# Loading and transposing the first head pair in halves, ahead of the centroids, in a clustered-attention and gated-feed-forward kernel

## The chip, the cores and the metric

The kernel runs on one core of a Trainium2 chip. The time is the device time of one execution in microseconds (us). Before the change the median of 7 runs is 344.58 us (343.99 to 345.71). A further execution was recorded by the hardware profiler; all durations and moments below come from that one, counted from the start of its span. The engines are TensorE (PE; its weight loads are listed apart as PEld), VectorE (DVE), ScalarE (ACT), GpSimd (POOL) and SyncE (SP), which here only issues DMAs.

## What is computed

Attention with routing by clusters, then a gated feed-forward network. There are 4 batches of 8 heads, 768 tokens, head size 64 and 16 centroids for each head. In short:

```python
q_assign = argmax(normalised(q) @ normalised(centroids).T)      # for each token and head, one of 16
k_assign = argmax(normalised(k) @ normalised(centroids).T)
scores   = q @ k.T / 8, and -1e9 where q_assign != k_assign
x        = softmax(scores) @ v                                  # heads side by side: 3072 x 512
xn       = x / sqrt(mean(x*x) + 1e-6) * rms_g
out      = (silu(xn @ w_gate) * (xn @ w_val)) @ w_out           # 512 -> 1536 -> 512
```

## The kernel before, in words

Heads are worked in 16 pairs. Each pair goes through a preparation whose parts `prep_parts` (L179) returns, and then through two *slots* of the main loop, one for each head.

The parts are named T0, T1, T2, T3, CAST, SP, TR, MX, CMP, SCL, BACK, PLACE and CASTV (L471). T0 to T3 are `t_group(g)` (L184) with g = 2 x head + side, side 0 for q and 1 for k: T0 is q of the first head, T1 is k of the first head, T2 is q of the second head, T3 is k of the second. Each makes three transposes of 128x128 float32 on TensorE (L194) into a PSUM tile tp, and then one copy of tp to one slice of the SBUF tile qk32 (L198 on VectorE, L200 on ScalarE; the line `on_dve` says which). A transposed group has tokens of even position in partitions 0 to 63 and of odd position in 64 to 127, so that CAST writes each group in two halves ("par" 0 and 1) as bfloat16 into aug, the operand of the score matmuls. For the first pair CAST reads PSUM (L211 on VectorE, L213 on ScalarE); for the others GpSimd does it (L217).

SP (`assign`, L225) multiplies the four slices of qk32 with the block-diagonal centroids cbd, four tiles side by side in the array, into PSUM (sp). TR, MX, CMP, SCL and BACK (L240 to L261) are five VectorE instructions, each reading what the one before wrote: transpose, maximum over the centroids, compare, scale, transpose back to ohT. PLACE (L264) sends ohT by four DMAs of 24 KB into rows 64 to 79 of the aug tiles; for the first pair one is issued by ScalarE, one by SyncE and two by GpSimd. So the score matmul sees both q·k and a large negative term where the clusters differ. CASTV copies v to bfloat16 on GpSimd (L222).

The order of everything is written out by hand (`manual_schedule`): an engine runs its instructions in the order of the program text. Before the main loop stand the loads, the centroid chain and the preparation of the first three pairs.

The loads: centroids on ScalarE's queue (L95); then on SyncE's queue q and k of pairs 0, 1 and 2 (each 384 KB: both heads), v of pair 0, and q of pair 3, which waits until T0 and T2 of pair 0 have been read because its buffer is that of pair 0 (three buffers for each of q, k and v).

The centroid chain (L139 to L146): sum of squares on VectorE, square root as a power on GpSimd (c_nm, L140), then on VectorE a reciprocal, a multiply-and-add, an add of 2e-6, a reciprocal and a scaling into c2. `put_centroids` (L148) transposes c2 on TensorE (c_ps) and copies it into cbd in two VectorE instructions (L152, L153), one for each half of the partitions, all eight heads at once.

`keep_warm(n)` (L126) issues n matmuls of 128x512 zeros, whose result is not used. The start in the program's order (L473 to L483):

```python
w_ps = keep_warm(9)
p0[T0](); p0[T2]()
keep_warm(2, w_ps)
put_centroids()
p0[T1](); p0[T3]()
p0[CAST]()
keep_warm(1, w_ps)
for i in (SP, TR, MX, CMP, SCL, BACK, PLACE):
    p0[i]()
```

Then come T0 to T3 of pair 1, two more loads, three warm-up matmuls, T0 to T3 and the casts around pair 2, five more warm-up matmuls, and the main loop (L546). A step of that loop makes a ninth of one slot's scores (L301; in the early slots three ninths at once, "scw"), their exponential on ScalarE (L304), a group of the product with v for the slot before (L315), and pieces of the feed-forward network of the batch before (L403, L436), and calls the parts of later pairs' preparation at steps listed in L496 to L541.

Of the kernel before, what the change touches and what calls it, by code (L numbers as in the profile page):

```python
# [8 lines left out]
F32 = mybir.dt.float32  # L9
BF16 = mybir.dt.bfloat16  # L10
AX = mybir.AxisListType.X
ALU = mybir.AluOpType
# [7 lines left out]
def kernel(  # L20
# [12 lines left out]
    nc = tc.nc  # L33
    B, H, S, D = q.shape
    NC = centroids.shape[1]
    DM, DF = moe_w_gate.shape
    P = 128
    ST = S // P
# [16 lines left out]
    const = ctx.enter_context(tc.tile_pool(name="const", bufs=1))  # L55
    ld = ctx.enter_context(tc.tile_pool(name="ld", bufs=3))
# [20 lines left out]
    loads = {}  # L77
# [9 lines left out]
    def load_pair(pi, kinds=range(3)):  # L87
        for kind in kinds:
            load_part(pi, kind)
# [3 lines left out]
    c_in = const.tile([P, D + 1], F32, name="c_in")  # L93
    nc.vector.memset(c_in[:, D:D + 1], 1e-15)
    nc.scalar.dma_start(out=c_in[:, 0:D], in_=centroids.rearrange("h c d -> (h c) d"))  # L95
    for pi in range(3):
        load_pair(pi, (0, 1))
    load_part(0, 2)
    load_part(3, 0)
# [6 lines left out]
    cbd = const.tile([P, H, NC, 2], F32, name="cbd")  # L106
# [19 lines left out]
    def keep_warm(n, w_ps=None):  # L126
        if w_ps is None:
            w_ps = ps_first.tile([P, CH], F32, name="w_ps", tag="f")
        for _ in range(n):
            nc.tensor.matmul(w_ps, lhsT=zeros[:, 0:P], rhs=zeros, start=True, stop=True)  # L130
        return w_ps
# [3 lines left out]
    c_ss = const.tile([P, 1], F32, name="c_ss")  # L135
    c_nm = const.tile([P, 1], F32, name="c_nm")
    c_t = const.tile([P, 1], F32, name="c_t")
    c2 = const.tile([P, 2, D], F32, name="c2")
    nc.vector.scalar_tensor_tensor(c_sq, c_in, 1.0, c_in, op0=ALU.mult, op1=ALU.mult, accum_out=c_ss)  # L139
    nc.gpsimd.tensor_tensor(c_nm, c_ss, half, op=ALU.pow)  # L140

    nc.vector.reciprocal(c_t, c_nm)
    nc.vector.scalar_tensor_tensor(c_t, c_t, c_ss, c_nm, op0=ALU.mult, op1=ALU.add)
    nc.vector.tensor_scalar_add(c_t, c_t, 2e-6)
    nc.vector.reciprocal(c_t, c_t)
    nc.vector.tensor_scalar_mul(c2, c_in[:, 0:D].unsqueeze(1).to_broadcast([P, 2, D]), c_t)  # L146

    def put_centroids():  # L148
        c_ps = ps_pv.tile([P, P], F32, name="c_ps", tag="acc")
        nc.tensor.transpose(c_ps, c2[:, :, :].rearrange("p a d -> p (a d)"), ident_f)  # L150
        c_pv = c_ps[:, :].rearrange("p (h c) -> p h c", c=NC)
        nc.vector.tensor_copy(cbd[0:D, :, :, 0], c_pv[0:D, :, :])  # L152
        nc.vector.tensor_copy(cbd[D:P, :, :, 1], c_pv[D:P, :, :])  # L153


    wg = const.tile([P, DC, DF], BF16, name="wg")
# [16 lines left out]
    def t_tile(name):  # L173
        pool, tag = ps_t, "t"
        if "wide" not in late:
            pool, tag = ps_first, "f"
        return pool.tile([P, HS], F32, name=name, tag=tag)

    def prep_parts(pi):  # L179
        st = pi % NSET  # L180
        qk32 = [None]
        state = {}

        def t_group(g):  # L184
            a, side = divmod(g, 2)
            if qk32[0] is None:
                qk32[0] = prep.tile([P, 4, HS], F32, name="qk32", tag="qk32", bufs=3)
            if pi == 2 and g > 1:
                tp = ((ps_t, ps_pv)[g - 2]).tile([P, HS], F32, name="tp", tag=("t", "acc")[g - 2])
            else:  # L190
                tp = t_tile("tp")
            src = loads[pi, side]
            for i in range(TH):
                nc.tensor.transpose(tp[:, i * P:(i + 1) * P], src[:, a, i * P:(i + 1) * P], ident_f)  # L194
            dst = qk32[0][:, g, :]
            on_dve = (g in (0, 3) if pi == 0 else g == 3 if pi == 2 else pi < 7 or g % 2)
            if on_dve:
                nc.vector.tensor_copy(dst, tp)  # L198
            else:
                nc.scalar.copy(dst, tp)  # L200
            state[g] = tp

        def casts():
            if pi == 0:
                for g in (0, 2, 1, 3):
                    a, side = divmod(g, 2)
                    for par in range(2):
                        dst = aug[0][a][0:D, side, par * HS:(par + 1) * HS]
                        src = state[g][par * D:(par + 1) * D, :]
                        if g == 3:  # L210
                            nc.vector.tensor_copy(dst, src)  # L211
                        else:
                            nc.scalar.copy(dst, src)  # L213
                return
            for a in range(2):
                for par in range(2):
                    nc.gpsimd.tensor_copy(aug[st][a][0:D, :, par * HS:(par + 1) * HS],  # L217
                                          qk32[0][par * D:(par + 1) * D, 2 * a:2 * a + 2, :])

        def casts_v():  # L220
            v_in = loads[pi, 2]
            nc.gpsimd.tensor_copy(vbf[st][:, :, :, 0:D],  # L222
                                  v_in[:, :, :].rearrange("p a (t d) -> p a t d", d=D))

        def assign():  # L225
            h0 = 2 * (pi % NP)
            if pi == 1:
                sp = ps_pv.tile([P, HS], F32, name="sp", tag="acc")
            else:
                sp = t_tile("sp")  # L230
            for j in range(4):
                side, a = divmod(j, 2)
                nc.tensor.matmul(sp[32 * j:32 * j + 32, :], lhsT=cbd[:, h0 + a, :, :].rearrange("p c r -> p (c r)"),  # L233
                                 rhs=qk32[0][:, 2 * a + side, :], start=True, stop=True,
                                 tile_position=(0, 32 * j))
            state["sp"] = sp

        def oh_tr():
            tr = prep.tile([P, HS], F32, name="tr", tag="tr")
            nc.vector.transpose(tr, state["sp"])  # L240
            state["tr"] = tr[:, :].rearrange("p (n c r) -> p n r c", c=NC, r=2)

        def oh_max():
            mx = small.tile([P, TH * 4, 2], F32, name="mx", tag="mx")
            nc.vector.tensor_reduce(mx, state["tr"], axis=AX, op=ALU.max)  # L245
            state["mx"] = mx

        def oh_cmp():
            oh = prep.tile([P, HS], BF16, name="oh", tag="oh")
            nc.vector.tensor_tensor(oh[:, :].rearrange("p (n c r) -> p n r c", c=NC, r=2), state["tr"],  # L250
                                    state["mx"].unsqueeze(3).to_broadcast([P, TH * 4, 2, NC]), op=ALU.is_ge)
            state["oh"] = oh

        def oh_scale():
            oh = state["oh"]
            nc.vector.tensor_scalar(oh[0:64, :], oh[0:64, :], scalar1=1.0, scalar2=MASK,
                                    op0=ALU.subtract, op1=ALU.mult)

        def oh_back():
            ohT = prep.tile([P, HS], BF16, name="ohT", tag="ohT")  # L260
            nc.vector.transpose(ohT, state["oh"])  # L261
            state["ohT"] = ohT

        def place():  # L264
            ohT = state["ohT"]
            for a in range(2):
                for side in range(2):
                    r = 32 * (2 * side + a)
                    eng = nc.sync
                    if pi == 0 and (side or not a):  # L270
                        eng = nc.gpsimd if side else nc.scalar
                    elif pi == 1 and (a or side):
                        eng = nc.gpsimd
                    eng.dma_start(out=aug[st][a][D:KA, side, :].rearrange("c (r n) -> c r n", r=2),
                                  in_=ohT[r:r + 2 * NC, :])

        return [lambda: t_group(0), lambda: t_group(1), lambda: t_group(2), lambda: t_group(3), casts, assign, oh_tr, oh_max, oh_cmp, oh_scale, oh_back, place, casts_v]


# [190 lines left out]

    T0, T1, T2, T3, CAST, SP, TR, MX, CMP, SCL, BACK, PLACE, CASTV = range(13)  # L471
    p0, p1, p2, p3 = (prep_parts(pi) for pi in range(4))
    w_ps = keep_warm(9)  # L473
    p0[T0]()
    p0[T2]()
    keep_warm(2, w_ps)
    put_centroids()
    p0[T1]()
    p0[T3]()
    p0[CAST]()  # L480
    keep_warm(1, w_ps)
    for i in (SP, TR, MX, CMP, SCL, BACK, PLACE):
        p0[i]()  # L483
    for i in (T0, T1, T2, T3):
# [3 lines left out]
    w_ps = keep_warm(3)  # L488
# [113 lines left out]
```

## Time and profile before

| | before |
|---|---|
| median of 7 runs | 344.58 us (343.99 to 345.71) |
| the profiled execution | 344.8 us |
| its span | 343.0 us |
| TensorE busy | 333.8 us (97%), 2957 matmuls |
| ScalarE busy | 225.8 us (66%) |
| VectorE busy | 222.4 us (65%) |
| GpSimd busy | 88.5 us (26%) |
| DMA | 34.99 MB, mean 102 GB/s |
| first score matmul starts | 14.89 us |

The profile has a page of totals, the chain of waits that ended last, followed back from the last instruction (line by line: start, length, what), a timeline of merged groups of instructions (start, length, engine, line, operation, operands, count, and in brackets the idle time before it with what ended it), and a list of DMA issues with the time from issue to landing. A group "x6" is six instructions in a row; its length runs from the first start to the last end. Matmuls overlap: a transpose is listed as 0.27 us or 0.42 us long, while the next one starts sooner. L numbers are lines of the kernel before the change.

### The profile page before, as it was taken

To read this page: it belongs to the slowest core of one execution; us is meant where nothing else is said; L and a number is where in the kernel's file an instruction comes from. 1 tells how busy PE (TensorE), PEld (TensorE's weight loads), DVE (VectorE), ACT (ScalarE), POOL (GpSimd) and SP (SyncE) were. 2 spreads that over 40 slices of the span, in tenths; PEclk is the share of its full clock that TensorE was granted. 3 is DMA by queue.
4 is the path that set the end of the run, shared out by engine and by line. 5 is a ranking of instruction groups with operands and counts; after the bars stand their busy time and mean duration, and the time that the engine had idled before them with its cause. 6 is when DMAs were issued, how large, how long until landed. Compare 5 with 4: busy or idle time off the path is not lost.

```text
span 343.0 us, 7541 instructions
## 1 busy us (share of the span) xinstructions
PE 333.8 (97%) x2957; PEld 203.7 (59%) x2957; DVE 222.4 (65%) x464; ACT 225.8 (66%) x392; POOL 88.5 (26%) x121
## 2 busy tenths in 40 slices
PE   8898999999999999999999999999999999999996
PEld 4556666667666565665656566566665655555553
DVE  4777787698765768766465668775555587655540
ACT  3588999978777586866767677777778343323322
POOL 1578696066441124231211304020000001000000
PEclk9999999999999999999999999999999999999999
DMA  7647999909843126161401002120000030300012
GB/s 263 211 143 247 235 249 245 266 14 156 224 152 110 71 52 176 44 183 39 151 28 42 32 11 68 45 56 32 32 1 32 32 78 32 78 31 31 32 62 92
DMA packets 36771, 34.99 MB, mean 102 GB/s; under 512 B 13520, under 2 KB 33664, under 8 KB 36736
## 3 DMA queue, kind: packets, MB, share of 16 engines
q1 hardware_dynamic: 30560, 29.62, 28.0%
q0 software_dynamic: 5984, 4.84, 9.0%
q8 instruction: 23, 0.38, 0.5%
q14 instruction: 12, 0.10, 0.1%
q10 hardware_dynamic: 192, 0.06, 0.1%
HBM read 28.61 MB, written 6.29 MB: 102 GB/s over the span
## 4 chain that ended last, share of the span: by engine, by line
PE 88%; DVE 7%; ACT 2%; issue 1%; DMA 1%; POOLq 0%; POOL 0%; DVEq 0%; ACTq 0%
PE gp L403 18%; PE vp L403 18%; PE dp L436 18%; PE sc L301 12%; PE acc L315 9%; PE tp L194 5%; PE sp L233 3%; PE scw L301 3%; ACT pT L304 2%; PE w_ps L130 1%; DVE oh L250 1%; DVE qk L198 1%; DVE tr L240 1%; DVE mx L245 1%; DMA aug<-ohT 1%
## 5 line engine op out<-in xcount | busy, mean ns | idle before, releaser
L304 ACT ACTIVATE pT<-sc 128x512 bf16<-128x512 f32 x192 | 113.7, 598 | 44.4 <-PE sc L301 44.0
L412 DVE SCALAR_TENSOR_TENSOR uu<-th,gp 128x384 f32<-128x384 f32 x96 | 53.1, 553 | 66.1 <-ACT th L408 65.9
L403 PE MATMUL vp<-xnT,wv 128*128 128x384 bf16 x384 | 78.1, 325 | 0.2 <-DVE gvT L418 0.2
L403 PE MATMUL gp<-xnT,wg 128*128 128x384 bf16 x384 | 78.1, 325 | 0.1
L436 PE MATMUL dp<-wo,gvT 128*128 128x512 bf16 (+1 forms) x300 | 75.9, 370 | 0.0
L408 ACT ACTIVATE th<-gp 128x384 f32<-128x384 f32 x96 | 47.3, 493 | 43.3 <-PE gp L403 40.6
L315 PEld LDWEIGHTS <-pT 128*128 128x128 bf16 x1152 | 57.0, 97 | 28.8 <-issue 2.5
L301 PE MATMUL sc<-aug 80*128 80x512 bf16 (+1 forms) x256 | 72.9, 326 | 0.0
L217 POOL CAST aug<-qk 64x768 bf16<-64x768 f32 x60 | 52.1, 869 | 53.5 <-DVE qk L198 36.9
L315 PE MATMUL acc<-vbf,pT 128*128 128x65 bf16 x1152 | 63.0, 194 | 0.6 <-ACT pT L304 0.2
L418 DVE TENSOR_TENSOR gvT<-uu,vp 128x384 bf16<-128x384 f32 x96 | 52.6, 548 | 6.1 <-PE vp L403 0.8
L403 PEld LDWEIGHTS <-wg 128*128 128x128 bf16 x384 | 37.2, 97 | 30.0 <-issue 0.4
L304 ACT ACTIVATE pT<-scw 128x1536 bf16<-128x1536 f32 x32 | 44.9, 1457 | 5.9 <-PE scw L301 5.5
L403 PEld LDWEIGHTS <-wv 128*128 128x128 bf16 x384 | 37.1, 97 | 18.6 <-issue 0.5
L436 PEld LDWEIGHTS <-gvT 128*128 128x128 bf16 x300 | 29.1, 98 | 24.4
L301 PEld LDWEIGHTS <-aug 80*128 80x128 bf16 x384 | 33.2, 97 | 16.3 <-issue 6.2
L198 DVE COPY qk<-tp 128x384 f32<-128x384 f32 x41 | 22.3, 552 | 15.4 <-PE tp L194 15.3
L301 PE MATMUL scw<-aug 80*128 80x512 bf16 (+1 forms) x128 | 26.0, 325 | 0.6 <-DMA aug<-ohT 0.4
L369 DVE SCALAR_TENSOR_TENSOR xn<-x,ir,g_b 128x512 bf16<-128x512 bf16 x24 | 20.2, 858 | 5.0 <-POOL ir L361 3.9
L222 POOL CAST vbf<-v_in 128x768 bf16<-128x768 f32 x16 | 13.4, 836 | 35.0 <-issue 34.6
L194 PE MATMUL tp<-ident_f,k_in 128*128 128x128 f32 x96 | 16.3, 282 | 2.5 <-DVE qk L198 2.2
L325 DVE TENSOR_TENSOR x<-acc,inv 128x384 bf16<-128x384 f32 x32 | 17.8, 558 | 1.1
(62 smaller groups left out, 196.2 us busy)
## 6 DMA issues: line engine op xcount, KB each, us to landing
q_in<-in_q_dram SPq DMA_DIRECT2D x16, 384.0 KB, 5.1
k_in<-in_k_dram SPq DMA_DIRECT2D x16, 384.0 KB, 5.4
v_in<-in_v_dram SPq DMA_DIRECT2D x16, 384.0 KB, 5.4
out_dram<-ob SPq DMA_DIRECT2D x23, 256.0 KB, 2.0
wg<-in_moe_w_gate_dram POOLq DMA_DIRECT2D x4, 384.0 KB, 8.8
wv<-in_moe_w_val_dram POOLq DMA_DIRECT2D x4, 384.0 KB, 10.7
wo<-in_moe_w_out_dram POOLq DMA_DIRECT2D x4, 384.0 KB, 7.2
aug<-ohT SPq DMA_DIRECT2D x58, 24.0 KB, 1.9
```

Source lines behind the costliest of these rows:

```text
L194: nc.tensor.transpose(tp[:, i * P:(i + 1) * P], src[:, a, i * P:(i + 1) * P], ident_f)
L198: nc.vector.tensor_copy(dst, tp)
L217: nc.gpsimd.tensor_copy(aug[st][a][0:D, :, par * HS:(par + 1) * HS], qk32[0][par * D:(par + 1) * D, 2 * a:2 * a + 2, :])
L301: nc.tensor.matmul(sc[:, o:o + n], lhsT=ag[:, 1, kc * P:(kc + 1) * P], rhs=ag[:, 0, qo:qo + n], start=True, stop=True)
L304: nc.scalar.activation(pts[slot][:, j * CH:(j + nch) * CH], sc[:, :nch * CH], ACT.Exp, scale=scale)
L315: nc.tensor.matmul(acc[:, TORD[g], :], lhsT=pts[slot][:, kc * S + g * P:kc * S + (g + 1) * P], rhs=vb[:, a, TORD[kc], :], start=(kc == 0), ...
L369: nc.vector.scalar_tensor_tensor(st["xn"][:, tl, :], x_t[b][:, t, :], st["ir", m][:, tl:tl + 1], g_b, op0=ALU.mult, op1=ALU.mult)
L403: nc.tensor.matmul(pt[:, :HS], lhsT=w[:, dc, fc * P:(fc + 1) * P], rhs=xnT[b, m][:, :, dc, :], start=(dc == 0), stop=(dc == DC - 1))
L408: nc.scalar.activation(th, pt[:, :HS], ACT.Tanh, scale=0.5)
L412: nc.vector.scalar_tensor_tensor(uu, th, 1.0, pt[:, :HS], op0=ALU.add, op1=ALU.mult)
L418: nc.vector.tensor_tensor(gvT[half][:, fc, :], uu, pt[:, :HS], op=ALU.mult)
L436: nc.tensor.matmul(dp, lhsT=gvT[hf][:, f, tl * P:(tl + 1) * P], rhs=wo[:, f, cols], start=(f == 0), stop=(f == FC - 1))
```

## The change

1. The first pair's q and k are loaded in four DMAs of 192 KB, one for each head and side, instead of two of 384 KB. The k of head 0 is issued by ScalarE behind the centroids, the other three by SyncE.
2. T0, T1, T2, T3 of pair 0 run in this order, all ahead of `put_centroids`, with 7 warm-up matmuls before T0, one after it, and 2 before SP (12 to 10 in all).
3. Of pair 0, only T3 is copied to qk32 by VectorE (T0 was too), and the casts run in the order of the groups; VectorE makes one cast (the second half of T3's group) instead of two, ScalarE seven instead of six.
4. `put_centroids` copies c_ps to cbd in four instructions: heads 0 and 1 for both halves of the partitions, then heads 2 to 7.
5. In the centroid chain, 2e-6 is added to c_nm by GpSimd (into c_ne), and the multiply-and-add takes c_ne; the add on VectorE is dropped.

```diff
-    for pi in range(3):
+
+    for kind, src in enumerate((q, k)):
+        loads[0, kind] = ld.tile([P, 2, ST * D], F32, name=("q_in", "k_in")[kind], tag=("q_in", "k_in")[kind])
+    for a in range(2):
+        for kind, src in enumerate((q, k)):
+            eng = nc.scalar if kind and not a else nc.sync
+            eng.dma_start(out=loads[0, kind][:, a, :], in_=src[0, a].rearrange("(p t) d -> p (t d)", p=P))
+    for pi in range(1, 3):
         load_pair(pi, (0, 1))
...
+    c_ne = const.tile([P, 1], F32, name="c_ne")
+    nc.gpsimd.tensor_scalar(c_ne, c_nm, scalar1=2e-6, scalar2=None, op0=ALU.add)
     nc.vector.reciprocal(c_t, c_nm)
-    nc.vector.scalar_tensor_tensor(c_t, c_t, c_ss, c_nm, op0=ALU.mult, op1=ALU.add)
-    nc.vector.tensor_scalar_add(c_t, c_t, 2e-6)
+    nc.vector.scalar_tensor_tensor(c_t, c_t, c_ss, c_ne, op0=ALU.mult, op1=ALU.add)
     nc.vector.reciprocal(c_t, c_t)
...
-        nc.vector.tensor_copy(cbd[0:D, :, :, 0], c_pv[0:D, :, :])
-        nc.vector.tensor_copy(cbd[D:P, :, :, 1], c_pv[D:P, :, :])
+        for hs in (slice(0, 2), slice(2, H)):
+            nc.vector.tensor_copy(cbd[0:D, hs, :, 0], c_pv[0:D, hs, :])
+            nc.vector.tensor_copy(cbd[D:P, hs, :, 1], c_pv[D:P, hs, :])
...
-            on_dve = (g in (0, 3) if pi == 0 else g == 3 if pi == 2 else pi < 7 or g % 2)
+            on_dve = (g == 3 if pi == 0 else g == 3 if pi == 2 else pi < 7 or g % 2)
...
-                for g in (0, 2, 1, 3):
+                for g in (0, 1, 2, 3):
...
-                        if g == 3:
+                        if g == 3 and par:
...
-    w_ps = keep_warm(9)
+    w_ps = keep_warm(7)
     p0[T0]()
+    keep_warm(1, w_ps)
+    p0[T1]()
     p0[T2]()
+    p0[T3]()
+    put_centroids()
+    p0[CAST]()
     keep_warm(2, w_ps)
-    put_centroids()
-    p0[T1]()
-    p0[T3]()
-    p0[CAST]()
-    keep_warm(1, w_ps)
     for i in (SP, TR, MX, CMP, SCL, BACK, PLACE):
         p0[i]()
```

## The prediction

> **What bounds the kernel now.** I read the page first, then the chain of waits from the start to 40 us, then the timeline, and last the DMA view issue by issue.
>
> ```profile
> span 343.0 us, 7541 instructions
> ...
> PE 88%; DVE 7%; ACT 2%; issue 1%; DMA 1%; POOLq 0%; POOL 0%; DVEq 0%; ACTq 0%
> ```
>
> TensorE carries 88% of the chain, and the change takes no matmul out of the main loops. So the change can pay only in the start-up, before the first score matmul, by as much as it moves that matmul. The start of the chain:
>
> ```profile
> 1.18 4.02 PE w_ps L130 x9
> 5.20 1.28 PE tp L194 x6
> 6.48 0.47 PE w_ps L130 x2
> 6.95 0.11 PE c_ps L150
> 7.06 0.67 PE tp L194 x6
> 7.73 0.02 issue
> 7.75 0.56 DVE qk L198
> 8.31 0.46 DVE aug L211
> ...
> 8.78 0.56 DVE aug L211
> ...
> 9.37 0.59 DVE tr L240
> ...
> 12.10 2.66 DMA aug<-ohT
> ...
> 14.89 0.81 PE scw L301 x4
> ```
>
> To be seen: up to 7.73 TensorE sets the pace. Then VectorE copies the last transposed group, casts it twice, and only then begins the run tr, mx, oh, oh, ohT (9.37 to 12.07), whose result goes by DMA into aug and releases the first scores at 14.89. From 9.37 on nothing in this chain is edited, so I price the change by the start of tr. The assignment matmuls (sp) end at 9.20, only 0.17 before tr.
>
> ```profile
> 4.94 1.14 PEld L194 LDWEIGHTS tp<-ident_f,q_in 128*128 128x128 f32 x6 [0.65 <-POOL c_nm L140]
> ...
> 7.10 0.28 DVE L152 COPY cbd<-c_ps 64x128 f32<-64x128 f32 x1 [0.63 <-PE c_ps L150]
> 7.40 0.31 DVE L153 COPY cbd<-c_ps 64x128 f32<-64x128 f32 x1
> 7.75 0.56 DVE L198 COPY qk<-tp 128x384 f32<-128x384 f32 x1
> 7.80 2.93 ACT L213 CAST aug<-tp 64x384 bf16<-64x384 f32 x6
> 7.86 1.34 PE L233 MATMUL sp<-qk,cbd 128*32 128x384 f32 x8
> ```
>
> The first transposes start at 4.94. The releaser that is printed is c_nm, but the transposes read q_in, and the DMA view has its landing:
>
> ```profile
> q_in<-in_q_dram SPq DMA_DIRECT2D x1, 384.0 KB, 4.1
> ```
>
> Issued at 0.73, it landed at 4.83, 0.11 before the weight load. The k load (issued 1.24, 4.6 us) landed at 5.84, the next q at 6.94. That is one 384 KB load per 1.0 us, 396 GB/s in the stretch from 3.5 to 4.5: the transfers queue for bandwidth.
>
> **The change, part by part.**
>
> *Loads.* The first q and k become four loads of 192 KB: q head 0 (SP), k head 0 (ACT, behind c_in), q head 1 and k head 1 (SP). Bytes are the same, so all four are down by 5.84. If they are served in the order of issue, they land half a microsecond apart: 4.33, 4.83, 5.34, 5.84. ACT's extra issue costs 0.44 (as c_in's) and pushes its table load from 1.19 to about 1.65; hidden, since ACT first works at 6.52. SP issues one load more before the second pair (0.5 us each): hidden, since those transfers wait for bandwidth and land a microsecond apart until 12.3 whenever they are issued; without that backlog it would cost 0.5 on pair 1.
>
> *TensorE.* Two spacings of one shape matter. The nine warm-up matmuls take 4.02 for the first 0.63 long: 0.424 apart. The five at 13.27 take 1.24 with 0.38 for one: 0.215 apart. Transposes stand likewise 0.214 apart in the q group (1.49 less 0.42, over 5) and 0.109 in the k group (0.82 less 0.27, over 5). The rate doubles between 6.27 and 6.57, in the two matmuls between those groups; I put it at 6.35. Seven warm-ups end at 1.18 + 7 x 0.424 = 4.15. T0 then waits for its half: 4.33 + 0.16 (as 4.83 to 4.99 now) = 4.49, after 0.34 idle. T0 to 5.13; one warm-up to 5.56; T1 (landed 4.83) to 6.20; T2 (landed 5.34) crosses the change of rate, to 6.58; T3 (landed 5.84) starts its last transpose at 6.80 and is done at 7.07. Now this last group is done at 7.71, so **T3 is 0.64 earlier**: 0.50 from the landing, the rest from two warm-ups and the centroid transpose (0.51 + 0.11) that no longer stand ahead of it, less the slow rate at which T1 now runs. Those three go behind T3 and end by 7.3, hidden by VectorE's work.
>
> *VectorE.* Now: copy (7.75; the next instruction follows 0.47 on), two casts (0.55 + 0.56), 0.03, tr: 1.62. After: copy 0.47, four cbd copies, one cast 0.56, 0.03. A cbd copy of 128 columns takes 0.30, a cast of 384 columns 0.55; a line through both gives 0.20 for 32 columns and 0.27 for 96, so the four cost 0.94. Bounds: 0.14 each if columns alone counted (0.60 in all), 0.30 each at worst (1.20). I take 0.94. So tr starts 2.00 after the copy: 7.07 + 0.04 + 2.00 = **9.11 against 9.37, a gain of 0.26**. The dropped cast and the two copies moved in nearly cancel the moved transposes. Cover: sp needs the first two cbd copies, done at 7.11 + 0.47 + 0.40 = 7.98; it takes 0.85 from one start when all operands are there (16 matmuls later in the trace: 15.63, 0.85), so it ends at 8.88, before VectorE is free. That it need not wait for all four copies is read from qk: sp starts at 7.86 while another slice of the same tile is being written until 8.31.
>
> *ScalarE.* It takes three copies and seven casts instead of two and six: copies at about 5.4, 6.4, 6.9, then 7 x 0.49, done near 10.7 as now. Its aug DMA waits for ohT (11.8) and is not delayed; the margin is 1.1, and with it gone one cast costs 0.49. Heads 0 and 1 of the casts in another order: nothing, slot 0's four end by 9.3.
>
> *Centroid chain.* One VectorE add of 0.19 start to start goes, but the next instruction now waits for a GpSimd add. Nearest row: GpSimd's 128x3 add at L360, 0.23. c_nm ends at 4.84, so the sum is there at about 5.2 where VectorE arrives at 5.07: zero net, bounds -0.19 and +0.3. Either way c2 is ready by 6.3 and c_ps starts after 6.9: hidden.
>
> *Later.* SP's next loads (at 12.88 and 13.46) and GpSimd's casts stand behind the aug DMAs and move with them. The main loop from 14.89 is released by those DMAs, so I carry the 0.26 to the end unchanged. The profiled execution took 344.8, span 343.0 plus 1.8 around it, 0.2 over the median: 344.8 - 0.26 = 344.54, and on the median 344.58 - 0.26 = **344.3**.
>
> **Two rules of the skill that speak against it.** The Trainium skill, DMA: Bandwidth & Descriptors, Issuing engines are not separate DMA queues, says that DMAs from several engines interleave on the same 16 DMA engines and that spreading them saves only issue time; by it the sum is rival B's, no gain. The Trainium skill, TensorE: Matmul & The Clock Gate, Part 1, has a free-running activity window of 3413 ns that must be busy before the clock doubles; the granted clock reads 1.00 throughout here, so only the spacings show it, and what an idle 0.34 does to such a window no trace here shows. By that rule the sum could be rival C's.
>
> **The rivals.**
>
> *B, the halves share the engines.* If k head 0 on ACT's queue takes every second turn from q head 0, both land at 4.83. T0 starts at 4.99 as now, T1 ends at about 6.53, T3 at 7.35, tr at 9.39: no gain, 344.6. For it: while c_in and q run together, c_in is not held back, though issued beside q (it lands 3.1 us after its issue). Against: k head 0 is issued 0.45 later.
>
> *C, slower: the rate of TensorE doubles later.* Now nothing interrupts TensorE from 1.18 to the doubling at 6.35. After, it stands idle for 0.34 (0.84 under B). If that idle time keeps the slow rate past 7 us, the loss begins there: T2 and T3 at 0.214, done at 7.69; copy 7.73; first two cbd copies 8.60; sp at half rate 1.70, to 10.35; tr at 10.42, 1.05 late: 345.6. With B's landing about 0.46 more: 346.1. For it: the slow rate holds for 5.2 us of unbroken work now. Against: later gaps (0.58 before 12.56, 0.38 before 14.89) leave the spacing fast.
>
> *D and E, collisions in the loop.* On the chain at 27.17 the oh compare took 1.12 instead of its median 0.59, and the scale at 28.33 took 0.73 instead of 0.25, beside GpSimd's casts. That is 1.02 us that a shift of 0.26 can undo (D: 344.3 - 1.0 = 343.3) or make a second time (E: 345.3; under B 345.6).
>
> *F, sp waits for all four cbd copies.* They end at 8.52; 0.05 + 0.85 + 0.07 gives tr at 9.49, 0.12 late: 344.7.
>
> **How the numbers follow.** Forecast 0.28, B 0.18, C 0.25, D 0.17, E 0.08, F 0.04. The bound of 0.3%, about what a measurement of this kernel can tell from no change, is 1.03 us: faster is below 343.55, slower above 345.61. Faster is D: 0.17. Slower is C but for its mildest tenth, and E where it meets B: 0.25. Within: 0.58. The range takes in D below and C alone above with the copies' bounds (0.3 either way): 343.2 to 345.9, leaving out C with B and what meets twice.
>
> **What would show it.** Right: the first q group's weight load near 4.5, the k group after one warm-up near 5.6, T3's copy on VectorE near 7.1, four cbd copies behind it of 0.2 to 0.27, tr near 9.1, first scores near 14.6. B: first weight load near 4.9. C: transposes of T2 and T3 still 0.21 apart, sp over 1.3 long. D or E: durations of oh between 20 and 35 us. The forecast falls if the first scores come earlier but a wait further on (the third pair's transposes behind GpSimd's casts at 30 us) takes it back, or if q head 0 lands after 4.9.

## The result and the profile after

| | before | after |
|---|---|---|
| median | 344.86 us (31 runs, 343.98 to 346.94) | 347.21 us (12 runs, 345.97 to 347.77) |
| the profiled execution, its span | 344.8 us, 343.0 | 347.42 us, 345.6 |
| ratio, 95% interval | | 1.0061 (1.0046 to 1.0076) |
| tr of pair 0 starts | 9.37 us | 10.67 us |
| first score matmul starts | 14.89 us | 16.18 us |
| mean granted clock of TensorE | 1.000 | 0.995 |

The kernel is slower by 0.6%, outside the range of the prediction. (The ratio is formed over the runs; the two medians alone would give 1.0068.) Two parts can be told apart at once in the profiles: the first scores come 1.29 us later, and the span is 2.6 us longer, so a second 1.3 us is lost after that. Line numbers from here on are those of the changed kernel, nine higher in most places (L249 is tr, L220 and L222 are the casts of pair 0 on VectorE and ScalarE, L310 the scores).

The page's totals and the chain's shares of the changed kernel:

```profile
span 345.6 us, 7541 instructions
...
PE 86%; DVE 8%; ACT 3%; issue 1%; DMA 1%; POOLq 0%; POOL 0%; DVEq 0%; ACTq 0%
```

The chain of waits of the changed kernel, from the start to the first scores (start, length, what):

```profile
1.18 3.17 PE w_ps L137 x7
4.34 0.64 PE tp L203 x3
4.98 0.43 PE w_ps L137
5.41 0.44 PE tp L203 x3
...
5.88 0.86 ACT qk L209 x2
6.74 0.36 ACT aug L222
...
9.57 0.48 ACT aug L222
...
10.08 0.56 DVE aug L220
...
10.67 0.59 DVE tr L249
...
13.39 2.65 DMA aug<-ohT
...
16.18 0.81 PE scw L310 x4
```

Before the change this chain went from TensorE straight to VectorE. Now ScalarE stands between them from 5.88 to 10.05, with its copies and casts, and VectorE's cast comes after the last of them. The timeline shows why:

```profile
6.53 0.56 DVE L207 COPY qk<-tp 128x384 f32<-128x384 f32 x1 [0.97 <-PE tp L203]
6.62 3.43 ACT L222 CAST aug<-tp 64x384 bf16<-64x384 f32 x7
7.01 0.17 DVE L161 COPY cbd<-c_ps 64x32 f32<-64x32 f32 x1
7.19 0.20 DVE L162 COPY cbd<-c_ps 64x32 f32<-64x32 f32 x1
7.42 0.25 DVE L161 COPY cbd<-c_ps 64x96 f32<-64x96 f32 x1
...
7.53 0.85 PE L242 MATMUL sp<-qk,cbd 128*32 128x384 f32 x8 [0.50 <-DVE cbd L162]
7.68 0.26 DVE L162 COPY cbd<-c_ps 64x96 f32<-64x96 f32 x1
...
10.08 0.56 DVE L220 CAST aug<-tp 64x384 bf16<-64x384 f32 x1 [2.13 <-ACT aug L222]
```

To be seen: VectorE has done the four cbd copies at 7.94, and the assignment matmuls are done at 8.38; tr could start then. But in VectorE's order its half cast of T3's group stands ahead of tr, and VectorE is idle for 2.13 us ahead of that cast, until ScalarE's seventh cast is over at 10.05. Both read the same PSUM tile, though not the same half of it: ScalarE's cast takes partitions 0 to 63, VectorE's 64 to 127. And ScalarE comes to this tile only at 9.57; from 7.94 to then it casts other groups. So what VectorE waits for is its turn, and not a memory that is being read.

The second part lies near 33 us. The wait of TensorE ahead of it, and then TensorE in steps of two microseconds (length, busy time and instructions, granted clock, share of DMA, GB/s), in the changed kernel:

```profile
32.07 0.55 PE L203 MATMUL tp<-ident_f,k_in 128*128 128x128 f32 x3 [1.63 <-DVE qk L207]
```

```profile
31.00:33.00 2.00, 0.93 (x11) 0.95 0.84 229
33.00:35.00 2.00, 2.00 (x19) 0.50 1.00 326
35.00:37.00 2.00, 2.00 (x26) 0.70 0.48 146
```

From 32.8 on TensorE is granted half its clock for 3.41 us, soon after 1.63 us in which it had stood waiting for a VectorE copy. Before the change the same wait is there and the clock stays at 1.00:

```profile
30.87 0.55 PE L194 MATMUL tp<-ident_f,k_in 128*128 128x128 f32 x3 [1.66 <-DVE qk L198]
```

```profile
31.70:33.70 2.00, 2.00 (x31) 1.00 0.86 259
```

Of the 12 runs after the change 9 have a mean clock of 0.995 and a median of 347.26; the other three, at 1.000, have 346.00. A mean of 0.995 is what one such stretch makes: half of 3.41 us is 0.5% of 345.6. Where the stretch lies can be seen only in the profiles, in this one and in two of the variants below; in all three it comes right after TensorE's idle time there.

### The profile page after: what moved, and what is told of

It is laid out like the page before. It is cut to its first block, busy times and chain, and to the rows that moved or that the text cites. A ratio compares the mean times of both kernels' runs of the same rounds, so it can differ in the third digit from the quotient of the medians.

```text
span 345.6 us, 7541 instructions
## 1 busy us (share of the span) xinstructions
PE 334.5 (97%) x2955; PEld 204.2 (59%) x2955; DVE 222.2 (64%) x463; ACT 226.5 (66%) x394; POOL 88.1 (25%) x122
## 4 chain that ended last, share of the span: by engine, by line
PE 86%; DVE 8%; ACT 3%; issue 1%; DMA 1%; POOLq 0%; POOL 0%; DVEq 0%; ACTq 0%
PE gp L412 18%; PE vp L412 18%; PE dp L445 17%; PE sc L310 12%; PE acc L324 8%; PE tp L203 5%; PE sp L242 3%; PE scw L310 3%; ACT pT L313 2%; DVE oh L259 1%; DVE qk L207 1%; PE w_ps L137 1%; DVE tr L249 1%; DVE mx L254 1%; DVE ohT L270 1%
## 5 line engine op out<-in xcount | busy, mean ns | idle before, releaser
L310 PE MATMUL sc<-aug 80*128 80x512 bf16 (+1 forms) x256 | 73.0, 327 | 0.0
L310 PEld LDWEIGHTS <-aug 80*128 80x128 bf16 x384 | 33.5, 98 | 16.4 <-issue 6.3
L310 PE MATMUL scw<-aug 80*128 80x512 bf16 (+1 forms) x128 | 26.9, 334 | 0.5 <-DMA aug<-ohT 0.4
L209 ACT COPY qk<-tp 128x384 f32<-128x384 f32 x24 | 11.2, 481 | 11.3 <-PE tp L203 7.1
```

The source lines that it names most:

```text
L310: nc.tensor.matmul(sc[:, o:o + n], lhsT=ag[:, 1, kc * P:(kc + 1) * P], rhs=ag[:, 0, qo:qo + n], start=True, stop=True)
```

## The experiments

Theory W: the first part is that one wait. Theory K: the second part is the stretch of half clock that follows TensorE's idle time near 30 us. The main rival of W is that the loads or the new order of the transposes cost the time. Each time stands against the kernel before on the same chip; "full clock" are runs whose mean granted clock is 0.998 or more.

**Both halves of T3's group on VectorE.**

```diff
-                        if g == 3 and par:
+                        if g == 3:
```

> The changed kernel, but both halves of T3's group are cast by VectorE, as before the change; all else is as changed. Theory W (the loss of the start is one wait: VectorE's half cast waits for ScalarE's seventh cast, and tr stands behind it): the wait goes, the casts follow the cbd copies at 7.95, tr starts near 9.1 instead of 10.67, the first scores near 14.6 instead of 16.2; if the granted clock is 1.00 throughout, about 344.6 us, else 1.2 more. Rival L (the loss comes from the loads and the order of the transposes): first scores stay near 16, time near 347.

345.31 us against 344.48, ratio 1.0022 (1.0003 to 1.0042). The wait is gone: the cbd copies end at 8.37, two casts follow at 8.38, tr starts at 9.54 and the first scores at 15.06. That is 1.1 earlier than in the changed kernel, and 0.45 later than expected, because T3 waited 0.35 for the second k load and its copy starts at 6.96 instead of 6.53. Six of the 12 runs are at 0.995; the six at full clock have 344.66, still 0.3 above those of before on that chip (344.37). W holds; L falls as the cause of the 1.3 us, though the loads do have a part in the 0.45.

**The kernel before, with the split cast alone.**

```diff
-                        if g == 3:
+                        if g == 3 and par:
```

> The kernel before, with one line of the change alone: VectorE casts only the second half of T3's group, ScalarE the first half (seven casts instead of six, in the old order). Theory W: ScalarE's seven casts run from 7.8 to 11.2, VectorE's waits for the last, tr starts near 11.8 instead of 9.37, the first scores near 17.3; 2.4 us slower than before, about 347.3, and more if a stretch of half clock is added. Rival L: VectorE casts once instead of twice, tr near 9.3 (the assignment matmuls end at 9.2), time as before, 344.9.

347.50 us against 344.48, ratio 1.0079 (1.0051 to 1.0108). One line alone, which takes work off VectorE, costs as much as the whole change does. In its timeline:

```profile
7.66 3.42 ACT L213 CAST aug<-tp 64x384 bf16<-64x384 f32 x7
...
11.11 0.56 DVE L211 CAST aug<-tp 64x384 bf16<-64x384 f32 x1 [2.94 <-ACT aug L213]
11.70 0.58 DVE L240 STREAM_TRANSPOSE tr<-sp 128x384 f32<-128x384 f32 x1
```

VectorE is idle for 2.94 us where the kernel before was idle for nothing; tr is at 11.70 (11.8 expected), the first scores at 17.20. Three of 6 runs are at 0.995 (348.52), three at full clock (346.44).

**All eight casts on ScalarE.**

```diff
-                        if g == 3 and par:
+                        if False:
```

> The changed kernel, but ScalarE makes all eight casts of the first pair and VectorE none. Theory W: no wait of VectorE on ScalarE is left, tr starts when the assignment matmuls end, near 8.45, the first scores near 14.0 (0.9 earlier than before the change), about 344.0 us; ScalarE's last cast ends near 10.6, ahead of ohT at 11.2. Rival L: first scores near 16, time near 347. A second rival (the later loop takes the gain back, or its stretch of half clock stays): first scores at 14.0 and the time still 344.9 or more.

345.76 us against 344.48, ratio 1.0018 (0.9998 to 1.0037). Read alone the median says that taking the wait out gains 1.5 us and no more; but 8 of 12 runs are at 0.995 (345.90) and the four at full clock have 343.76, 0.6 below the full-clock runs of before on that chip (344.37). In the profile tr waits for nothing but the assignment matmuls, and ScalarE's eighth cast is over at 11.04, ahead of ohT:

```profile
7.13 3.91 ACT L222 CAST aug<-tp 64x384 bf16<-64x384 f32 x8
...
9.28 0.58 DVE L249 STREAM_TRANSPOSE tr<-sp 128x384 f32<-128x384 f32 x1 [0.50 <-PE sp L242]
```

tr is 0.8 later than the 8.45 expected, since in this execution TensorE's rate doubled late: T1, T2 and T3 (5.21, 5.88, 6.51) each take 0.82 to 0.87, against 0.49 to 0.63 in the profile of the changed kernel. The same is seen in the kernel before: by the trace's record of the clock the rate doubles at 6.43 in its profile and at 5.33 in that of its filled control further down, with tr at 9.37 and at 8.83, though the two programs differ only in matmuls that run at 28.95 and later. Single profiles are to be compared with this half microsecond in mind.

**The first half on VectorE, the second on ScalarE.**

```diff
-                        if g == 3 and par:
+                        if g == 3 and not par:
```

> The changed kernel, but VectorE casts the first half of T3's group and ScalarE the second, so that of the two it is ScalarE that comes later. The work of each engine is that of the changed kernel. Theory W (the wait is one of order between two engines that read the same PSUM tile): VectorE's cast follows the cbd copies at 7.95, tr near 8.55, the first scores near 14.1, about 344.1 us if the clock stays at 1.00. Rival L, or a rival by which one cast more on ScalarE is what costs: first scores near 16, time near 347.

344.24 us against 344.48, ratio 0.9997 (0.9975 to 1.0019); eight runs at full clock have 344.01. The work on each engine is that of the changed kernel; only which engine comes later is turned round, and 3 us of median go (4 of 12 runs are still below full clock). The cast follows the cbd copies without a gap:

```profile
8.56 0.55 DVE L220 CAST aug<-tp 64x384 bf16<-64x384 f32 x1
...
9.05 0.58 DVE L249 STREAM_TRANSPOSE tr<-sp 128x384 f32<-128x384 f32 x1
```

First scores at 14.56 (14.1 expected; T3 waited 0.66 for the second k load). Two rivals fall with it: that a seventh cast on ScalarE costs the time, and that the loads do.

**The idle time near 30 us filled, in three kernels.** Four matmuls of zeros are issued after the score chunk of step 27, into the score tile that the next chunk overwrites:

```diff
+    def fill(n):
+        late["next"] = late["wide"].tile([P, WCH * CH], F32, name="scw", tag="scw")
+        for _ in range(n):
+            nc.tensor.matmul(late["next"][:, 0:CH], lhsT=zeros[:, 0:P], rhs=zeros, start=True, stop=True)
...
-            sc = late["wide"].tile([P, WCH * CH], F32, name="scw", tag="scw")
+            sc = late.pop("next") if "next" in late else late["wide"].tile([P, WCH * CH], F32, name="scw", tag="scw")
...
+    at(27, lambda: fill(4))
```

> The changed kernel with four matmuls of 512 columns of zeros more, issued after the score chunk of loop step 27, into the score tile that the next chunk overwrites: they lie in the stretch near 30 to 32 us in which TensorE waits for a VectorE copy. Theory K (beside the wait, most of the changed kernel's runs lose 1.2 us more to 3.4 us of half clock that follow this idle stretch): the granted clock is 1.000 in every run, the median near 346.0, 1.5 over before, first scores still at 16.2. Rival (the half clock comes from something else, such as the shorter start): clock 0.995 as often as without the fill, median near 347.2.

346.24 us against 344.59, ratio 1.0044 (1.0029 to 1.0059). All 8 runs are at full clock. The wait is still there (1.76 us idle ahead of the cast, in the first line below), and so are 1.65 us of loss; what went is the other 1.0 (347.21 to 346.24). The second line is the filling, of which this profile has three of the four matmuls:

```profile
9.76 0.56 DVE L220 CAST aug<-tp 64x384 bf16<-64x384 f32 x1 [1.76 <-ACT aug L222]
```

```profile
30.42 1.02 PE L318 MATMUL scw<-zeros 128*128 128x512 bf16 x3 [0.30 <-ACT pT L313]
31.77 0.55 PE L203 MATMUL tp<-ident_f,k_in 128*128 128x128 f32 x3 [0.33 <-DVE qk L207]
```

The kernel with all casts on ScalarE, filled:

> The changed kernel with all eight casts on ScalarE and the same four matmuls of zeros after step 27. Theories W and K together: no wait of VectorE on ScalarE and no half clock, so every run is like the full-clock runs of the kernel with all casts on ScalarE, 343.7 to 344.2: median near 343.8, 0.6 below before. Rival: the fill delays the second transpose group of pair 4 or the score chunk behind it, and the median is 344.3 or more.

344.29 us against 344.59, ratio 0.9987 (0.9975 to 0.9998); 12 of 12 at full clock. It was expected at 343.8; the gain over before is half of what was expected, and the interval ends just below 1. 344.3 was the mark of the rival, that the filling delays what follows. In the profile the transposes behind the filling still wait 0.31 us for the VectorE copy, so no delay is seen there.

The kernel before, filled, as a control:

> The kernel before with the same four matmuls of zeros after step 27. Theory K: its 6 runs of 29 at clock 0.995 go, and since they are few the median falls only from 344.5 to about 344.3. Rival: the fill has a cost or a gain of its own, then the full-clock runs, 343.6 to 345.1 without it, move.

344.72 us against 344.59, ratio 1.0005 (0.9994 to 1.0016); 12 of 12 at full clock. Its full-clock runs are no faster than without the filling (344.72 against 344.52), so the filling has no gain of its own; the half clock that it takes away is seldom there on this chip (2 of 31 runs). With the filling the full-clock runs are 0.2 slower here, 0.2 in the changed kernel (346.24 against 346.00) and 0.5 with all casts on ScalarE (344.29 against 343.76); these were not all taken on one chip, but a small cost of its own can't be ruled out.

**All casts on ScalarE, with the old loads.** The first pair's loads are those of the kernel before. (Line numbers of this kernel: L197 is the transposes.)

> The changed kernel with all eight casts on ScalarE, but the first pair loaded as before the change, in two loads of 384 KB on one queue. It prices the split loads. By the prediction's step (the first half lands 0.5 us earlier) T0 starts near 4.9 instead of 4.14, T3 ends and tr starts 0.3 to 0.6 later than with the split loads (8.5 to 9.3 there), the first scores near 15.0. Rival (T0 is bound by the seven warm-up matmuls and T3 by the second k load, which land alike): no difference, first scores 14.6 to 14.8. At full clock 344.0 to 344.4 by the first, 343.8 by the second; some half-clock runs 1.5 to 2 us above.

344.28 us against 344.59, ratio 1.0001 (0.9982 to 1.0021). T0 waits for its load:

```profile
4.59 0.87 PE L197 MATMUL tp<-ident_f,q_in 128*128 128x128 f32 x3 [0.25 <-DMA q_in<-in_q_dram]
```

That is 0.45 later than with the split loads (4.14). The first scores are at 14.47, not later than with them (14.79 and 14.60 in the two profiles), for the second half of k lands no earlier in the split form. Eight full-clock runs have 344.14. With the split loads four on another chip have 343.76, and the twelve with the filling on this chip 344.29: no gain of the split loads is shown.

**VectorE's half cast read from SBUF.** The changed kernel, filled, with the operand of the one cast exchanged:

```diff
                         if g == 3 and par:
-                            nc.vector.tensor_copy(dst, src)
+                            nc.vector.tensor_copy(dst, qk32[0][par * D:(par + 1) * D, g, :])
```

> The changed kernel with the four matmuls of zeros after step 27 and one edit more: VectorE's half cast reads its operand from qk32 (the copy in SBUF that VectorE made itself) instead of the PSUM tile tp that ScalarE's cast reads as well. Both engines still write halves of the same aug tile, and the number of casts of each engine is that of the changed kernel. If the wait comes from two engines reading one PSUM tile: no wait of VectorE on ScalarE, tr between 8.4 and 9.2 (by the moment at which TensorE's rate doubles), first scores 13.9 to 14.7, median near 344.3, 2.0 below the changed kernel with the fill. If it comes from two engines writing one aug tile: wait of 1.8 to 2.1 as before, first scores near 16, 346.2.

343.90 us against 344.72, ratio 0.9972 (0.9954 to 0.9990). The wait is gone, and both engines still write the same aug tile. So it belongs to the PSUM tile that both read in the changed kernel:

```profile
6.97 3.43 ACT L222 CAST aug<-tp 64x384 bf16<-64x384 f32 x7
...
8.09 0.26 DVE L162 COPY cbd<-c_ps 64x96 f32<-64x96 f32 x1
8.38 0.36 DVE L220 CAST aug<-qk 64x384 bf16<-64x384 f32 x1
...
8.85 0.58 DVE L249 STREAM_TRANSPOSE tr<-sp 128x384 f32<-128x384 f32 x1
```

First scores at 14.11. The cast is also shorter (0.36 against 0.56), so this is a little more than the change as it was meant. It has the lowest median of all versions, 0.8 us below before (0.7 below the full-clock runs of before on that chip, 344.58) and 2.3 below the changed kernel with the filling; its interval overlaps with that of all casts on ScalarE.

**The kernel before, filled, with all casts on ScalarE.**

```diff
-                        if g == 3:
+                        if False:
```

> The kernel before with the four matmuls of zeros after step 27 and all eight casts of the first pair on ScalarE (old loads, old order). It tells what the rest of the change is worth once the wait is out of it: the changed kernel in this form has 344.29. VectorE's two casts go, but the assignment matmuls end only 0.1 to 0.2 before VectorE would be free, so tr is at most 0.2 earlier than with them: 344.6 against 344.72. So the rest of the change would be worth about 0.3. Rival: ScalarE's eight casts end too late for its aug DMA and the time rises over 344.7.

344.22 us against 344.72, ratio 0.9985 (0.9962 to 1.0009); 344.6 was expected. tr starts at 9.18, when the assignment matmuls end. With the rest of the change this form had the ratio 0.9987: in this form the new loads and the new order are worth nothing that these runs can tell. Two of its 12 runs are at clock 0.994 in spite of the filling, so the filling doesn't always keep the clock up.

## Why the prediction was wrong

*The step that failed* is the VectorE term, "two casts (0.55 + 0.56), 0.03, tr ... After: copy 0.47, four cbd copies, one cast 0.56, 0.03". It has the right instructions and no wait between them. Splitting T3's group gave two engines one PSUM tile to read, one after the other, and the order of issue made VectorE the later one: behind ScalarE's seven casts. The numbers to price it were in the prediction: VectorE at the cast near 8.5, ScalarE "done near 10.7". Their difference, 2.2, is the wait, 2.13 us in the profile; without it tr would have come at 8.54 there, and not at 10.67. I wrote of ScalarE's casts only that their end leaves 1.1 to ScalarE's own DMA, and of their order only that heads 0 and 1 the other way round cost "nothing". Nothing in the page of before shows such a wait, because there it costs nothing: ScalarE's first cast at 7.80 reads the tile of T0 that VectorE had copied by 6.47. The rule that I asked of every other added instruction, who stands behind it on its engine, was not asked of an instruction that stayed while its partner moved to another engine. A second step failed beside it: the main loop was taken at an unchanged clock, and the 9 of 12 runs with the half clock have a median 1.26 higher than the other three.

*The rest of the sum.* The version with the same work on each engine and no wait (the first half on VectorE) has tr at 9.05, where the prediction had 9.11, and its full-clock runs are 0.36 below those of before, where it had 0.26; the ratio of all runs, 0.9997, can't tell that from nothing. That the two figures lie so near is in part luck: T3's transposes are done at 7.10 there, against 7.07 in the sum, but with T0 0.35 earlier than forecast, the rate doubled at 4.93 and a wait of 0.66 for k, none of which the sum has. That the shift of the start is carried on unchanged held as far as 32 us: from the first scores to the transposes behind the long wait it is 15.98 us before and 15.89 after.

*Loads.* The first half of q came much earlier than forecast: it landed 2.5 us after its issue, at 3.2, not at 4.33, so T0 was released by the end of the seven warm-up matmuls at 4.14, and not by its load. Then came the second half of q (about 4.0) and the first of k (about 4.3), which were issued within 0.03 us of each other; the forecast had these two the other way round. The second half of k took 4.1 us (landed 5.74), and in four of the profiles of the variants T3 waited 0.17 to 0.93 for it. The forecast had all four down by 5.84; in the seven profiles with split loads the last is down at 5.4 to 6.5, in the five with the old loads at 5.3 to 5.8. So the split brings the first piece early and the last one no earlier, often later. Rival B fell: k on ScalarE's queue doesn't delay the first q. The Trainium skill (DMA: Bandwidth & Descriptors, Issuing engines are not separate DMA queues) says that DMAs of several engines interleave on the same 16 DMA engines and that a second issuing engine saves only issue time. The landing of the last piece does not speak against it. What the prediction made of it, no gain at T0, is not what was measured: T0 started at 4.14 instead of 4.99.

*TensorE.* There was no idle time ahead of T0, and the rate doubled during T1, at 5.48, so rival C did not arise in the form that I gave it. Something like it did, elsewhere: half the rate after idle time, near 33 us, with 1.26 us between the medians of the 9 runs that have it and the 3 that don't. I had read the later gaps as evidence that idle time does not harm the clock; the profiled execution of before has the same wait near 30 us without the half clock, and I had only that one. The Trainium skill (TensorE: Matmul & The Clock Gate, Part 1) has the window of 3413 ns; the stretch of half clock in the trace is 3.41 us long, which agrees. The idle time ahead of it is 1.63 us, about half of such a window.

*VectorE's cbd copies* took 0.17, 0.20, 0.25 and 0.26, against 0.20 and 0.27 in the sum (whose lower bound of 0.14 each does not quite make the 0.60 beside it; nothing rests on that). Rival F fell: the assignment matmuls start at 7.53, while the third and fourth copies run until 7.94. *The GpSimd add* made VectorE wait 0.16, hidden. *D and E*: the slow pair at 27.17 and 28.33 came again at 28.39 and 29.54, with 1.12 and 0.72, and in all the other profiles with 1.10 to 1.12 and 0.73: an earlier or a later start shifts it as a whole.

*What stays open.* Why the half clock follows in 9 of 12 runs after the change and in 14 of 83 of before, when the idle stretch is 1.63 and 1.66 us in the two profiles. With the filling 44 of 44 runs of four kernels were without it, where the changed kernel unfilled had 3 such runs of 12; then 2 of 12 of a fifth had it again. So that the stretch matters is shown, and what sets how often is not.

The traces have a lead, which no run tests. Their record of the clock begins when the rate doubles (what the views print as 1.00 ahead of that is the lack of a record): at 5.48 us in the changed kernel, at 7.17 with all casts on ScalarE, at 6.15 in before with the split cast. These are the three profiles with a half clock, and it begins 27.31, 23.89 and 27.31 us later, which is 8, 7 and 8 times 3.413. Count steps of 3.413 us from the doubling: in these three, one step holds all of the idle time near 30 us, and the half clock begins at its end. In the four unfilled profiles that keep the clock a border of two steps falls into that idle time or between its pieces; in before it is at 30.33, and the idle time runs from 29.21 to 30.87. By that the moment of doubling, which differs from execution to execution, would decide. But it is not the whole rule: in the changed kernel with the filling 1.67 us of idle time (11.86 to 13.54) lie inside one step (11.65 to 15.06), and no half clock follows.

## What to carry to other kernels

When work is moved from one engine to another, look for the tiles that both now touch, reading too, and ask which comes later in the text: the later one takes over the earlier one's whole queue, and everything behind it on its own engine waits along. If two engines must share a PSUM tile, let the engine that the critical path needs come first, or give it a copy of its own to read. And where executions of one kernel differ by a constant amount, set the granted clock of each run beside its time before the medians are compared: here it was worth as much as the edits.

## What was not expected of the hardware

A stretch of half clock of 3.41 us in TensorE after some 1.6 us of idle time, with 1.3 to 2.1 us between the medians of the runs without and with it (346.00 against 347.26 in the changed kernel, 343.76 against 345.90 with all casts on ScalarE). At half rate 3.41 us can cost TensorE at most 1.7, so in the second kernel something else goes with it, or its four runs at full clock are too few. And a cast of 64x384 took 0.36 us on VectorE from SBUF where from PSUM it took 0.56.
